# Zero products ahead of the first transform, paired butterflies, quartered fifth denominators and another tail order in a two-headed attention and Fourier kernel

## The chip, the cores and the metric

The kernel runs on one core of one Trainium2 chip. The metric is the device time of one execution in microseconds. Three runs of the kernel before gave 710.68, 712.03 and 708.92 us; their median is 710.68 us. A smaller time is better.

## The reference

Two independent computations share one launch, and their results stand side by side in the output (2048 x 1152).

```python
def _A_ref(x, wq, wk, wv, wo, beta):          # x: 1 x 2048 x 576, 32 heads of 18, 4 segments of 512
    q, k, v = heads(x @ wq), heads(x @ wk), heads(x @ wv)
    M = 0; z = 0
    for s in range(4):
        p = softmax(qs @ ks.T * scale + causal mask); a_dot = p @ vs
        pq = phi(qs); num = pq @ M; den = pq @ z + 1e-6
        outs.append(g * num / den + (1 - g) * a_dot)
        M = M + phi(ks).T @ vs;  z = z + phi(ks).sum(rows)
    return concat(outs) @ wo
def _B_ref(x, w_r, w_i):                      # x: 1 x 2048 x 576
    return irfft2(rfft2(x) * (w_r + 1j * w_i), s=(2048, 576))
```

Here phi(t) is t+1 for positive t and exp(t) otherwise, and g is the sigmoid of beta.

## The kernel before, in words

The order of the instructions on each engine is the order in which the Python code emits them: the tile framework's own scheduling is off. Every engine works through its own list in order. Generators are advanced by hand so that work of one part lies between work of another. The stages, by the profile's time, are:

- **Forward transform, 0 to 71 us** (class FFT, `forward`, L103 to L198). The 2048 rows are taken as 16 blocks of 128 (`u` = 0 to 15). For each block SyncE loads `xin`; `prep` (L121) forms sum and difference `eo` on VectorE, rounds them on ScalarE into `eh`, and forms the rest `el` on VectorE. `eh` lives in three buffers whose third part holds zeros beside 33 written rows; GpSimd clears these parts at the start (L166). `f1` (L136) multiplies the block with the table `ftab` on TensorE, 14 products for one block: for each of two results `r` two with the first half of the table, two with its second half, and two with `el`, and one with the small table `ftab2`. GpSimd issues the loads of the first half, the second half and `ftab2` (L170 to L173), after the clearing. The result is copied to `X` by ScalarE (L147) and VectorE (L150), multiplied by the twiddle matrices `cfw` (`c1`, L155, 12 products) and stored in `Z`. The loop at L181 emits this for `u`, `u-1` and `u-3` side by side.
- **Length-16 part of the transform on VectorE, spread over 36 to 324 us.** `bf` (L200) is a butterfly of four complex tiles of 2 x 290 elements, ten VectorE instructions: six on 580 elements and four on 290. `tws` (L211) multiplies by a twiddle: two ScalarE scalings of 580 (L218, L219) and two VectorE instructions of 290 (L224, L226) for one tile. `stage1` does this for each of four groups, `middle` runs a butterfly, the multiplication by the filter `W`, the inverse butterfly and the twiddles, and `last` one more butterfly. There are 16 butterflies and 18 twiddled tiles. A counter (`Pace`) hands their steps out: one or two for a block in the forward transform, and then an equal share for each unit of the projections.
- **Projections, 71 to 271 us** (L548). For each of four segments `g` nine units of q and k (`qk_unit`, L466) and four of v. In a q/k unit TensorE makes 14 products into `pj`, ScalarE and VectorE split the result into three bfloat16 parts `sp` (L477, L484, L491), TensorE subtracts the second part (L493), and ScalarE makes the third (L494).
- **Inverse transform, 271 to 350 us** (`inverse`, L285), with the first scores beside it.
- **Attention, 350 to 660 us** (L954). For each of 128 pairs of a segment and a head TensorE makes scores `s`, VectorE takes maxima, ScalarE exponentials `P`, and TensorE the products with v. Background generators run between them; one of them is `den` (L779), called three times. It multiplies `zst`, the sums of phi(k) laid out for five groups of heads `t`, with `pq` = phi(q): four groups into the four sets of 32 output rows of one accumulator `pd`, which ScalarE copies to `ds`; in its next step the fifth group into 32 rows of a new accumulator, with a copy of its own. SyncE then writes `ds` to memory, from where `recip` reads it back.
- **Tail, 660 to 708 us** (end of `attention`). Eight accumulators (`u`: four row blocks, two halves of 288 columns) collect the last output projection. `last_proj(u,t)` (L902) adds the three products of head group `t`. The parts `t`<4 are emitted for `u`<7, then for `u`=7; then a loop adds `t`=4 to each `u`, copies the half on ScalarE or VectorE (L1047), and after each second one SyncE writes a row block of 576 columns (L1048).

Of the kernel before, what the change touches and what calls it, by code (L numbers as in the profile page):

```python
# [5 lines left out]
F32=mybir.dt.float32; F32R=mybir.dt.float32r  # L6
AF=mybir.ActivationFunctionType; OP=mybir.AluOpType
# [95 lines left out]
class FFT:  # L103
# [4 lines left out]
    def forward(s,xp,cp,pp,wl,xs,consts):  # L108

        nc,io=s.nc,s.io; v=nc.vector  # L110
# [25 lines left out]
        def f1(u):  # L136
            p=pp.tile([128,2,512],F32,name="f1",tag="f1")
            h,l=eh.pop(u),el.pop(u)
            for r in range(2):
                L=[(h[:,r,0],tab[:,0,r,0]),(h[:,r,1],tab[:,0,r,1]),(h[:,r,0],tab[:,1,r,0]),(h[:,r,1],tab[:,1,r,1]),  # L140
                   (l[:,r,0],tab[:,0,r,0]),(l[:,r,1],tab[:,0,r,1]),(l[:99,r,2],tab2[:99,r])]
                for n,(x,t) in enumerate(L):
                    nc.tensor.matmul(p[:,r,:FP],x,t,start=n==0,stop=n==6)  # L143
            F[u]=p
        def ev0(u):
            x=xp.tile([128,2,FP],F32R,name="X0",bufs=3); X[u]=[x]
# [16 lines left out]
                        nc.tensor.matmul(p[:,r,:FP],cc[:,hl,k*128:(k+1)*128],x[i][:,q],start=n==0,stop=n==5)  # L163
                        n+=1
        H=[xp.tile([128,2,3,128],F32R,name=f"eh{i}",bufs=1) for i in range(3)]
        for h in H: nc.gpsimd.memset(h[:,:,2].bitcast(F32),0.0)  # L166
        load(0)
        tab=cp.tile([128,2,2,2,FP],F32R,name="ftab",bufs=1)
        tab2=cp.tile([128,2,FP],F32R,name="ftab2",bufs=1)
# [7 lines left out]
        for i in range(2):  # L177
            for x in p: next(x)
        load(3)
        s.pace=Pace(61+165+40)  # L180
        for u in range(20):  # L181
            p=prep(u+2) if u+2<16 else iter(())
            if 0<u<17: ev0(u-1)
# [12 lines left out]
            if u>13: s.pace.take(2)  # L196
        for _ in wl: pass
        for _ in xs: pass  # L198
    def bf(s,x,y,inv):

        v=s.nc.vector; tp=s.tp
        t=[tp.tile([128,2,FP],F32,name=f"t{i}",tag="t",bufs=8) for i in range(4)]
        p,m=(y[1],y[3]) if not inv else (y[3],y[1])
        for o,a,b,op in ((t[0],x[0],x[2],OP.add),(t[1],x[0],x[2],OP.subtract),(t[2],x[1],x[3],OP.add),(t[3],x[1],x[3],OP.subtract),
                         (y[0],t[0],t[2],OP.add),(y[2],t[0],t[2],OP.subtract),
                         (p[:,0],t[1][:,0],t[3][:,1],OP.add),(p[:,1],t[1][:,1],t[3][:,0],OP.subtract),
                         (m[:,0],t[1][:,0],t[3][:,1],OP.subtract),(m[:,1],t[1][:,1],t[3][:,0],OP.add)):
            v.tensor_tensor(o,a,b,op=op)  # L208
            yield
    def tws(s,L,inv):  # L210

        nc=s.nc; v=nc.vector; A=[]; L=[x for x in L if x[1]]
        if not L: return
        for i in range(len(L)+1):
            if i<len(L):
                y,e=L[i]; a=-2*np.pi*e/16*(-1 if inv else 1)
                t=[s.tp.tile([128,2,FP],F32,name=f"tw{k}",tag="t",bufs=8) for k in range(2)]
                nc.scalar.activation(t[0],y,AF.Copy,scale=float(np.cos(a)))  # L218
                nc.scalar.activation(t[1],y,AF.Copy,scale=float(np.sin(a)))  # L219
                A.append((y,t))  # L220
                if i==0: yield
            if i>0:
                y,t=A.pop(0)
                v.tensor_tensor(y[:,0],t[0][:,0],t[1][:,1],op=OP.subtract)  # L224
                yield
                v.tensor_tensor(y[:,1],t[0][:,1],t[1][:,0],op=OP.add)  # L226
                yield
    def stage1(s,b):
        x=[s.Z[:,b,a] for a in range(4)]
        yield from s.bf(x,x,False)  # L230
        yield from s.tws([(x[c],b*c) for c in (2,1,3)],False)
    def middle(s,wp):
        nc,io=s.nc,s.io; v=nc.vector
        Ws=[]
        def ld(i):
            W=wp.tile([128,2,FP],F32,name="W",bufs=3)
            nc.sync.dma_start(W,io["w"][i//4][:,i%4])
            Ws.append(W)
        for i in range(3): ld(i)
        for c in range(4):  # L240
            x=[s.Z[:,b,c] for b in range(4)]
            yield from s.bf(x,x,False)
            for d in range(4):
                W=Ws[4*c+d]
                t=s.tp.tile([128,2,FP],F32,name="wm",tag="t",bufs=8)
                t2=s.tp.tile([128,2,FP],F32,name="wm2",tag="t",bufs=8)
                v.tensor_tensor(t,x[d],W[:,0][:,None,:].to_broadcast([128,2,FP]),op=OP.mult)
                yield
                v.tensor_tensor(t2,x[d],W[:,1][:,None,:].to_broadcast([128,2,FP]),op=OP.mult)
                if 4*c+d+3<16: ld(4*c+d+3)  # L250
                yield
                v.tensor_tensor(x[d][:,0],t[:,0],t2[:,1],op=OP.subtract)
                yield
                v.tensor_tensor(x[d][:,1],t[:,1],t2[:,0],op=OP.add)
                yield
            yield from s.bf(x,x,True)
            yield from s.tws([(x[b],b*c) for b in (2,1,3)],True)
    def inv_setup(s,cp):
        nc,io=s.nc,s.io
        s.cp=cp; s.civ={}  # L260
# [9 lines left out]
    def last(s):  # L270

        for b in range(4):
            x=[s.Z[:,b,c] for c in range(4)]
            yield from s.bf(x,x,True)
# [69 lines left out]
BF=mybir.dt.bfloat16  # L344
# [43 lines left out]
class ATT:  # L388
# [123 lines left out]
    def v_unit(s,g,tb,tp,pp):  # L512
        nc=s.nc
        P=[]
        for hf in range(2):
            ps=pp.tile([128,288],F32,name="pjv",tag="pj")
            yield from s.passes(ps,g,"wv",slice(288*hf,288*hf+288),slice(128*tb,128*tb+128),True)
            P.append(ps)
            yield
        vt=tp.tile([128,622],F32,name="vt")  # L520
        vv=vt[:,:608].rearrange("p (h c) -> p h c",c=19)
        nc.gpsimd.memset(vv[:,:,18:19],1.0)  # L522
        nc.gpsimd.memset(vt[:,608:],0.0)
# [12 lines left out]
        n=g+1  # L536
        for t in range(5):
            w=7 if t<4 else 4; r=18*w
            m=tp.tile([126,7,19],F32,name="mm")
            nc.vector.tensor_tensor(m[:r,:w],s.pm[t//3][:r,t%3,:w],s.bm[:r,:w],op=OP.mult)  # L540
            M=s.Mst[n][:r,t,:r].rearrange("p (h c) -> p h c",c=18)
            z=s.zst[n][:r,t,:w]
            if n==1:
                nc.gpsimd.tensor_copy(M,m[:r,:w,:18])
                nc.gpsimd.tensor_copy(z,m[:r,:w,18])
            else:
                nc.gpsimd.tensor_tensor(M,m[:r,:w,:18],s.Mst[g][:r,t,:r].rearrange("p (h c) -> p h c",c=18),op=OP.add)
                nc.gpsimd.tensor_tensor(z,m[:r,:w,18],s.zst[g][:r,t,:w],op=OP.add)  # L548
    def projections(s,xp,tp,pp,wv,pace,hook):

        live=[]
# [6 lines left out]
        tot=pace.left-10  # L558
# [221 lines left out]
        s.pq[g,t]=x  # L780
    def den(s,g,lane):
        nc=s.nc; tp=s.tp
        ds,ds2=[tp.tile([128,512],F32,name=f"ds{i}",tag="ux",bufs=3) for i in range(2)]; ds2=ds2[:32]
        for T,d in ((range(4),ds),((4,),ds2)):
            pd=s.post("pd")
            for t in T:
                r=126 if t<4 else 72
                nc.tensor.matmul(pd[32*(t%4):32*(t%4)+32],s.zst[g][:r,t],s.pq[g,t][:r],start=True,stop=True,skip_group_check=True)
            nc.scalar.copy(d,pd[:d.shape[0]])
            yield  # L790
        for t in range(5):
            w=7 if t<4 else 4
            s.later(1,lambda t=t,w=w: nc.sync.dma_start(s.dD[g][7*t:7*t+w],ds[32*t:32*t+w] if t<4 else ds2[:w]))
# [147 lines left out]
    def attention(s,tp,ps):  # L941
# [6 lines left out]
        m=None  # L948
# [89 lines left out]
                if t==2 and u in (1,4): s.last_tile(3 if u==1 else 4,"rd")  # L1038
        s.last_low()
        for u in range(7): s.last_proj(u,3)  # L1040
        for t in range(4): s.last_proj(7,t)
        o=[s.tp.tile([128,4,512],F32,name=f"P{i}").rearrange("p a b -> p (a b)") for i in range(2)]
        o=[o[tb//3][:,576*(tb%3):576*(tb%3)+576] for tb in range(4)]
        nc=s.nc
        for u in range(8):
            tb,hf=divmod(u,2); s.last_proj(u,4)
            (nc.vector.tensor_copy if hf else nc.scalar.copy)(o[tb][:,288*hf:288*hf+288],s.acc[u])  # L1047
            if hf: nc.sync.dma_start(s.io["ya"][1536+128*tb:1664+128*tb],o[tb])  # L1048

def prio(tc,gen,off):  # L1050

# [104 lines left out]
```

## Time and profile before

| | |
|---|---|
| runs | 710.68, 712.03, 708.92 us (median 710.68) |
| profiled execution, own time | 709.86 us |
| its span, first to last instruction | 708.2 us |
| TensorE busy | 678.8 us, 96% of the span |
| VectorE busy | 544.8 us, 77% |
| ScalarE busy | 455.8 us, 64% |
| GpSimd busy | 194.6 us, 27% |
| granted TensorE clock, mean | 0.999 |

In the profile PE is TensorE (matmuls), PEld its weight loads, DVE VectorE, ACT ScalarE, POOL GpSimd and SP SyncE. A row of the timeline gives start, duration, engine, line, instruction, the tiles written and read, their shapes and the number of merged instructions; in brackets stands the idle time before it and what ended it. Durations of successive instructions overlap, so the distance between starts is what one of them costs the engine. A row of the table by windows gives for each engine the busy time in that stretch and the number of instructions, then the granted clock, the busy share of the DMA engines and the moved GB/s.

### The profile page before, as it was taken

The page shows a single profiled execution, that of the slowest core. Times are in us where ns is not written, and L with a number is a line of the kernel's source. Part 1 is how long each engine was busy: PE and PEld are TensorE (multiplying, and loading weights), DVE is VectorE, ACT ScalarE, POOL GpSimd, SP SyncE. Part 2 cuts the span into 40 slices and gives each one's busy share as a digit, 9 for nine tenths or more (in the row PEclk, how much of TensorE's full clock was granted, in tenths as well). Part 3 has the DMA queues.
Part 4 walks back from the last instruction along what each step waited for, and adds up shares of the span by engine and source line. Part 5 has one row for each costly group of instructions (what it writes and reads, how often), then busy time and mean ns, then how long its engine had stood idle before and what let it go on. Part 6 is the DMA issues. An engine that isn't in the chain of part 4 may idle for free.

```text
span 708.2 us, 14408 instructions
## 1 busy us (share of the span) xinstructions
PE 678.8 (96%) x4991; PEld 501.3 (71%) x4991; DVE 544.8 (77%) x1258; ACT 455.8 (64%) x1004; POOL 194.6 (27%) x392
## 2 busy tenths in 40 slices
PE   4999999999999999999999899999999999998997
PEld 3999769879779879998954454445566445663587
DVE  4899969899699789797787787988657876567533
ACT  3777796585686484544388777777656776567421
POOL 3111000100200102665135333444233752235310
PEclk9999999999999999999999999999999999999999
DMA  9897355666384679999338976976766766442151
GB/s 328 256 305 202 115 141 187 186 185 202 100 250 156 178 196 311 202 240 267 100 114 210 190 163 143 207 182 167 154 129 181 182 166 154 92 122 65 29 164 74
DMA packets 71146, 123.80 MB, mean 175 GB/s; under 512 B 12184, under 2 KB 39174, under 8 KB 67482
## 3 DMA queue, kind: packets, MB, share of 16 engines
q1 hardware_dynamic: 64422, 106.89, 57.4%
q0 software_dynamic: 5632, 15.76, 8.2%
q8 instruction: 39, 0.64, 0.4%
q10 hardware_dynamic: 1020, 0.25, 0.2%
q14 instruction: 33, 0.27, 0.1%
HBM read 82.10 MB, written 39.81 MB: 172 GB/s over the span
## 4 chain that ended last, share of the span: by engine, by line
PE 68%; DMA 8%; ACT 4%; DVE 4%; POOL 2%; issue 2%; SPq 0%; ACTq 0%; DVEq 0%; POOLq 0%
PE pj L464 12%; PE pv L734 9%; PE s L656 9%; PE pjv L464 8%; PE po L877 6%; PE i L309 3%; PE i L298 3%; PE s L705 3%; PE s L709 2%; DMA yb<-yout 2%; PE pn L807 2%; PE s L669 2%; PE pm L532 2%; PE s L714 2%; DMA Ks<-qkD 1%
## 5 line engine op out<-in xcount | busy, mean ns | idle before, releaser
L664 DVE CUSTOM_DVE_ANT_0 junk<-s,x 128x512 bf16<-128x512 f32 x248 | 137.0, 552 | 58.0 <-PE s L656 52.6
L719 POOL TENSOR_SCALAR_AFFINE_SELECT P<-P 128x512 f32<-128x512 f32 (+2 forms) x132 | 78.5, 626 | 112.9 <-ACT P L706 104.1
L670 DVE TENSOR_REDUCE mx<-s 128x4 f32<-128x512 f32 x128 | 87.7, 685 | 5.6 <-PE s L669 3.7
L706 ACT ACTIVATE P<-s 128x512 f32<-128x512 f32 x128 | 77.7, 607 | 10.8 <-PE s L705 3.8
L734 PE MATMUL pv<-P,vs 128*32 128x512 f32 (+3 forms) x1024 | 82.5, 439 | 0.1
L715 ACT ACTIVATE P<-s 128x256 f32<-128x256 f32 x128 | 49.8, 389 | 46.1 <-PE s L714 45.7
L711 ACT ACTIVATE P<-s 128x512 f32<-128x512 f32 x128 | 77.4, 605 | 2.4 <-PE s L710 2.2
L656 PE MATMUL s<-Ks,Qs 108*128 108x384 bf16 (+3 forms) x256 | 69.1, 301 | 1.5 <-DMA ux<-uD 1.0
L734 PEld LDWEIGHTS pv<-P,vs 128*32 128x32 f32 x1024 | 26.9, 109 | 45.3 <-issue 35.1
L464 PE MATMUL pj<-x,wqkh 128*128 128x512 f32 x162 | 56.5, 409 | 0.0
L208 DVE TENSOR_TENSOR Z<-t,t 128x290 f32<-128x290 f32 (+1 forms) x96 | 48.4, 553 | 0.1
L656 PEld LDWEIGHTS <-Qs 108*128 108x128 bf16 x320 | 31.5, 98 | 23.5 <-issue 12.1
L208 DVE TENSOR_TENSOR t<-Z 128x580 f32<-128x580 f32 x64 | 46.1, 755 | 0.0
L669 PE MATMUL s<-tri,idb 128*128 128x128 bf16 x256 | 43.0, 219 | 0.0
L522 POOL MEMSET vt<- 128x32 f32 x16 | 2.3, 162 | 141.3 <-PE pm L532 119.5
L298 PE MATMUL i<-civ,Y 128*128 128x256 f32 (+1 forms) x288 | 39.3, 289 | 0.2 <-POOL Y L283 0.2
L298 PEld LDWEIGHTS i<-civ,Y 128*128 128x128 f32 (+1 forms) x288 | 36.5, 181 | 1.0 <-POOL Y L283 0.4
L309 PE MATMUL i<-itab,T 128*128 128x290 f32 (+1 forms) x224 | 36.7, 306 | 0.5 <-DVE yout L317 0.4
L464 PE MATMUL pj<-x,wqkl 128*128 128x512 f32 x90 | 35.6, 395 | 0.0
L464 PE MATMUL pj<-xh,wqkl 128*128 128x512 f32 x90 | 35.5, 395 | 0.0
L143 PE MATMUL f<-ftab,eh 128*128 128x290 f32 x128 | 25.3, 321 | 10.7 <-DMA ftab<-ftab 10.6
L464 PE MATMUL pj<-xh,wqkh 128*128 128x512 f32 x90 | 35.5, 395 | 0.0
(210 smaller groups left out, 1806.3 us busy)
## 6 DMA issues: line engine op xcount, KB each, us to landing
qkD<-sp SPq DMA_DIRECT2D x32, 384.0 KB
xin<-xb SPq DMA_DIRECT2D x16, 384.0 KB
cfw<-cfw POOLq DMA_DIRECT2D x16, 384.0 KB, 4.7
civ<-civ POOLq DMA_DIRECT2D x16, 384.0 KB, 9.0
vs<-vD SPq DMA_DIRECT2D x16, 330.0 KB
vD<-vt SPq DMA_DIRECT2D x16, 311.0 KB
W<-w SPq DMA_DIRECT2D x16, 290.0 KB
yb<-yout SPq DMA_DIRECT2D x16, 290.0 KB
```

Source lines behind the costliest of these rows:

```text
L208: v.tensor_tensor(o,a,b,op=op)
L298: nc.tensor.matmul(p[:m,k],Y[i][:,q,c*128:c*128+m],cc[:,hl,o:o+256],start=n==0,stop=n==5)
L309: nc.tensor.matmul(p,x,t,start=n==0,stop=n==6)
L464: s.nc.tensor.matmul(out,a,b,start=i==0,stop=i==len(L)-1)
L656: nc.tensor.matmul(out,Q[:108,h,128*i:128*i+128],K[:108,h,:128*(i+1)],start=True,stop=True)
L664: nc.vector.tensor_tensor_reduce(out=junk[:,:w],in0=src,in1=s.mask[:,512-w:],scale=1.0,scalar=-3.0e38, op0=OP.add,op1=OP.max,accum_out=s.m ...
L669: nc.tensor.matmul(pa[:,o+w-128:o+w],s.idb,s.tri,start=False,stop=True,skip_group_check=True)
L670: nc.vector.tensor_reduce(out=s.mx[k][:,hh],in_=pa.rearrange("p (b c) -> p b c",c=128),axis=mybir.AxisListType.X,op=OP.max)
L706: nc.scalar.activation(P[0][:,hh],p0,AF.Exp,scale=SC)
L711: nc.scalar.activation(P[1][:,hh],p1,AF.Exp,scale=SC)
L719: nc.gpsimd.affine_select(out=x[:,r],in_=x[:,r],pattern=[[0,r.stop-r.start],[1,128]],compare_op=OP.is_ge,fill=0.0,base=0,channel_multiplie ...
L734: nc.tensor.matmul(s.pvt[32*hh:32*hh+32,128*j:],vt[:,j,19*h:19*h+32],mv[0][:,hh,mv[1]],start=j==0,stop=j>1,skip_group_check=True)
```

## The change

1. VectorE, not GpSimd, clears the three `eh` parts, after clearing a new tile `z`. TensorE multiplies `z` with itself 26 times ahead of the first transform, into a buffer of `c1`, and five times more inside block 0.
2. In block 0 the four products with the first half of the table come first for both results; then the five zero products; then the rest.
3. A butterfly writes its last two results with one instruction of 2 x 290 each (the third part is read in reverse order), so that it has eight instructions and not ten. Where a twiddle is a quarter turn (two tiles), the butterfly's subtraction does it, in two halves. The other 16 twiddled tiles have two ScalarE scalings of 290 and one VectorE `scalar_tensor_tensor` of 580. The counter's totals fall from 266 to 216.
4. The fifth group of denominators is added into the accumulator of the first four: columns 8 to 11 of each set of 32 rows, a quarter of the 512 query columns in each. One copy is left; SyncE writes the fifth group in four pieces.
5. In the tail the `t`<4 part of `u`=7 stands after `u`=5 is finished, and the last row block is written in two halves.

```diff
         def f1(u):
...
+            O=[(r,n) for r in range(2) for n in range(7)]
+            if u==0: O.sort(key=lambda a: a[1]>1)
+            for i,(r,n) in enumerate(O):
+                x,t=L[r][n]
+                nc.tensor.matmul(p[:,r,:FP],x,t,start=n==0,stop=n==6)
+                if u==0 and i==3: zeros(5)
...
-        for h in H: nc.gpsimd.memset(h[:,:,2].bitcast(F32),0.0)
+        z=xp.tile([128,512],BF,name="z",bufs=1)
+        v.memset(z,0.0)
+        def zeros(n):
+            for i in range(n): nc.tensor.matmul(zp[:,0],z[:,:128],z,start=True,stop=True)
+        for h in H: v.memset(h[:,:,2].bitcast(F32),0.0)
...
+        zp=pp.tile([128,2,512],F32,name="c1",tag="c1")
+        zeros(26)
-        s.pace=Pace(61+165+40)
+        s.pace=Pace(44+140+32)
...
     bf:
+        L=[(t[0],x[0],x[2],OP.add),(t[1],x[0],x[2],OP.subtract),(t[2],x[1],x[3],OP.add),(t[3],x[1],x[3],OP.subtract),(x[0],t[0],t[2],OP.add)]
+        if turn:
+            g,h=(t[2],t[0]) if inv else (t[0],t[2])
+            L+=[(y[:,0],g[:,1],h[:,1],OP.subtract),(y[:,1],h[:,0],g[:,0],OP.subtract)]
+        else: L+=[(y,t[0],t[2],OP.subtract)]
+        L+=[(s.slots(p,m+1),t[1],t[3][:,::-1],OP.add),(s.slots(m,p+1),t[1],t[3][:,::-1],OP.subtract)]
...
     tws:
+                for k in range(2): nc.scalar.activation(t[:,k],y[:,1-k],AF.Copy,scale=float((-np.sin(a),np.sin(a))[k]))
...
+                nc.vector.scalar_tensor_tensor(z,z,c,x,op0=OP.mult,op1=OP.add)
...
     den:
+        for t in range(4): nc.tensor.matmul(pd[32*t:32*t+32],s.zst[g][:126,t],s.pq[g,t][:126],start=True,stop=False,skip_group_check=True)
+        for j in range(4):
+            c=slice(128*j,128*j+128)
+            nc.tensor.matmul(pd[32*j:32*j+32,c],s.zst[g][:72,4],s.pq[g,4][:72,c],start=False,stop=True,skip_group_check=True)
+        nc.scalar.copy(ds,pd)
...
-        for t in range(4): s.last_proj(7,t)
...
+            if u==6:
+                for t in range(4): s.last_proj(7,t)
...
+            if hf or u>5: nc.sync.dma_start(s.io["ya"][1536+128*tb:1664+128*tb,c],o[tb][:,c])
```

TensorE's list begins with block 0 of the forward transform. Before, with `f` the accumulator, `eh` and `el` the block's parts and `ftab` the table:

```order
L143 MATMUL f_167<-ftab,eh_112 128x290 x4
L143 MATMUL f_167<-ftab,el 128x290 x2
L143 MATMUL f_167<-ftab_121,el 128x290
L143 MATMUL f_167<-ftab,eh_112 128x290 x4
L143 MATMUL f_167<-ftab,el 128x290 x2
L143 MATMUL f_167<-ftab_121,el 128x290
```

After it begins as follows (the pair of load and product with `z` stands 26 times ahead of `f` and five times behind its first four products):

```order
L172 LDWEIGHTS z
L172 MATMUL c_162<-z 128x512
L145 MATMUL f_196<-ftab,eh_112 128x290 x4
...
L145 MATMUL f_196<-ftab,eh_112 128x290 x2
L145 MATMUL f_196<-ftab,el 128x290 x2
L145 MATMUL f_196<-ftab_123,el 128x290
```

The four products that need only the first half of the table now come ahead of everything that needs the second half or the small table.

Also on TensorE, in the attention stage, the first call of `den` before (the scores `s` between its two steps make up 20 rows, the products with v two):

```order
L788 MATMUL pd<-pq,zst_67 32x512 x4
L656 LDWEIGHTS Qs_3306
L656 MATMUL s_5677<-Ks_3307,Qs_3306 128x256
...
L734 MATMUL pv<-P_5444,vs 32x384 x4
L734 MATMUL pv<-P_5445,vs 32x256 x4
L788 MATMUL pd<-pq,zst_67 32x512
```

And after:

```order
L722 MATMUL s_5625<-Qs_3267,x_2721 128x128
L797 MATMUL pd<-pq,zst_67 32x512 x4
L800 MATMUL pd<-pq,zst_67 32x128 x4
L668 LDWEIGHTS Qs_3268
L668 MATMUL s_5640<-Ks_3269,Qs_3268 128x256
```

The single product of 512 columns behind the products with v has become four of 128 columns directly behind the first four.

On VectorE, in the projections of segment 0, the end of the third group of `stage1` before, with `tw` the scaled copies, `pj`, `sp` and `ex` the work of the projection units and `xl`, `wvl` splits of loaded data:

```order
L208 TENSOR_TENSOR Z<-t_1050,t_1052 128x290
L410 TENSOR_TENSOR wvl<-raw,wvh 64x288
L437 TENSOR_TENSOR xl<-xst,xh 128x512
L224 TENSOR_TENSOR Z<-tw_1163,tw_1164 128x290
L483 SCALAR_TENSOR_TENSOR ex<-pj,ex 128x512
L484 TENSOR_TENSOR pj<-pj,sp_1183 128x512
L226 TENSOR_TENSOR Z<-tw_1163,tw_1164 128x290
L224 TENSOR_TENSOR Z<-tw_1188,tw_1189 128x290
L226 TENSOR_TENSOR Z<-tw_1188,tw_1189 128x290
```

And after:

```order
L225 TENSOR_TENSOR Z<-t_1018,t_1020 128x2x290 x2
L421 TENSOR_TENSOR wvl<-raw,wvh 128x288 x2
L448 TENSOR_TENSOR xl<-xst,xh 128x512
L495 TENSOR_TENSOR pj<-pj,sp_1140 128x512
L237 SCALAR_TENSOR_TENSOR Z<-Z,tw 128x580
L421 TENSOR_TENSOR wvl<-raw,wvh 128x288
L421 TENSOR_TENSOR wvl<-raw,wvh 64x288
L237 SCALAR_TENSOR_TENSOR Z<-Z,tw 128x580
L494 SCALAR_TENSOR_TENSOR ex<-pj,ex 64x512
```

The four halves of a butterfly's end have become two instructions, a twiddled tile has one and not two, and the third group's twiddles stand one to two units earlier.

More of the change, by code (lines that the diff above doesn't have):

```diff
@@ L240, in middle @@
         for c in range(4):
-            x=[s.Z[:,b,c] for b in range(4)]
-            yield from s.bf(x,x,False)
+            I=[8*b+2*c for b in range(4)]; x=[s.slots(i,i+1) for i in I]
+            yield from s.bf(I,False)
             for d in range(4):
@@ L255, in middle @@
                 yield
-            yield from s.bf(x,x,True)
-            yield from s.tws([(x[b],b*c) for b in (2,1,3)],True)
+            yield from s.bf(I,True,c==2)
+            if c: yield from s.tws([(I[b],b*c) for b in (2,1,3) if b*c!=4],True)
     def inv_setup(s,cp):
@@ L272, in last @@
         for b in range(4):
-            x=[s.Z[:,b,c] for c in range(4)]
-            yield from s.bf(x,x,True)
+            yield from s.bf([8*b+2*c for c in range(4)],True)
             s.done=b
@@ L557, in advance @@
                 except StopIteration: live.remove(l)
-        tot=pace.left-10
+        tot=pace.left-8
         for g in range(4):
@@ L782, in den @@
         nc=s.nc; tp=s.tp
[L783 to L793, printed above, removed]
+        ds=tp.tile([128,512],F32,name="ds",tag="ux",bufs=3)
+        pd=s.post("pd")
+        for t in range(4): nc.tensor.matmul(pd[32*t:32*t+32],s.zst[g][:126,t],s.pq[g,t][:126],start=True,stop=False,skip_group_check=True)
[3 more added lines that the diff above has]
+        nc.scalar.copy(ds,pd)
+        yield
+        for t in range(4):
+            s.later(1,lambda t=t: nc.sync.dma_start(s.dD[g][7*t:7*t+7],ds[32*t:32*t+7]))
+        for j in range(4):
+            s.later(1,lambda c=slice(128*j,128*j+128),j=j: nc.sync.dma_start(s.dD[g][28:32,c],ds[32*j+8:32*j+12,c]))
+        yield
         def chain():
```

59 lines of the change are left out of this document (25 added, 34 removed).

## The prediction

> **What bounds the kernel now.** I read the busy times first, then the waits of TensorE stage by stage, then the timeline where it waits.
>
> ```profile
> PE 678.8 (96%) x4991; PEld 501.3 (71%) x4991; DVE 544.8 (77%) x1258; ACT 455.8 (64%) x1004; POOL 194.6 (27%) x392
> 40.00:60.00 20.00, 19.88 (x140) 18.75 (x139) 19.92 (x32) 14.82 (x27) 3.34 (x7) 1.00 0.85 258
> 90.00:110.00 20.00, 18.33 (x98) 14.55 (x97) 14.46 (x27) 18.74 (x36) 0.00 (x0) 1.00 0.51 140
> 110.00:271.00 161.00, 160.29 (x925) 136.81 (x924) 139.40 (x261) 106.05 (x207) 14.26 (x60) 1.00 0.63 186
> ```
>
> TensorE is the bound nearly everywhere. So an edit pays where it takes TensorE's own work away, where TensorE waits, or ahead of its first and behind its last product. Work taken from VectorE or ScalarE pays only where these are full: VectorE from 40 to 60 us (19.92 of 20), ScalarE from 90 to 110 us (18.74 of 20).
>
> The opening is the largest hole. TensorE's rows, and one of its weight loads:
>
> ```profile
> 9.62 0.82 PE L143 MATMUL f<-ftab,eh 128*128 128x290 f32 x2 [9.62 <-DMA ftab<-ftab]
> 11.38 0.85 PE L143 MATMUL f<-ftab,eh 128*128 128x290 f32 x2 [0.93 <-DMA ftab<-ftab]
> 12.66 0.29 PEld L143 LDWEIGHTS f<-ftab,el 99*128 99x128 f32 x1 [0.31 <-DMA ftab<-ftab]
> 13.07 1.17 PE L143 MATMUL f<-ftab,eh 128*128 128x290 f32 x4
> 14.77 1.17 PE L143 MATMUL f<-ftab,eh 128*128 128x290 f32 x4
> 16.46 1.03 PE L143 MATMUL f<-ftab,eh 128*128 128x290 f32 x4
> 17.72 0.71 PE L143 MATMUL f<-ftab,eh 128*128 128x290 f32 x4
> 21.52 1.79 PE L163 MATMUL c<-X,cfw 128*128 128x290 f32 x12
> 37.22 0.70 PE L143 MATMUL f<-ftab,eh 128*128 128x290 f32 x4
> 40.73 0.69 PE L143 MATMUL f<-ftab,eh 128*128 128x290 f32 x4
> ```
>
> It waits 9.62 us for the first half of the table, 0.93 for the second, and then runs slowly: seven products take 1.70 us (13.07 to 14.77), 0.243 each. Later a block's 26 products (14 of `f`, 12 of `c`) take 3.51 us (37.22 to 40.73), 0.135 each. The granted clock reads 1.00 in the windows, so that column does not show it; the distances do. Four products have 1.03 us at 16.46 and 0.71 at 17.72: the fast rate comes at about 16.9 us, 5.5 us after the last gap.
>
> **The opening in the change.** A product of 512 bfloat16 columns at the fast rate costs 0.22 us:
>
> ```profile
> 508.20 0.38 PE L705 MATMUL s<-Qs,x 110*128 110x512 bf16 x1
> 508.42 0.38 PE L656 MATMUL s<-Ks,Qs 108*128 108x512 bf16 x1
> 0.81 0.81 POOL L166 MEMSET eh<- 128x256 f32 x3 [0.29 <-POOLq L1143]
> 1.56 0.72 POOL L170 DMA_DIRECT2D ftab<-ftab  x1
> ```
>
> Slowly it would cost 0.22 x 0.243/0.135 = 0.40 us. The zero products wait for `z`, cleared from about 0.8 to 1.2 us if VectorE is about as quick as GpSimd (0.81 us for three). Fourteen slow ones fill the 5.5 us until 6.7, twelve fast ones 2.6 us more: they end at 9.3 us, just ahead of the table's 9.62. Behind them four products (0.54) and five zeros (1.1) reach 11.3; the second half lands at 11.38, the small table at 12.66. The last six of block 0 then end at about 13.6 us, not 14.77. Three more blocks of 14 x 0.135 = 1.89 us end at 19.3, where `c` stood at 21.52: TensorE gains 2.2 us. `z` holds one of two `c1` buffers until 11.3; the second `c` comes long after.
>
> What is late next is VectorE, which forms `el`:
>
> ```profile
> 13.62 1.03 DVE L126 TENSOR_TENSOR eo<-xin 128x384 f32<-128x384 f32 x2 [1.21 <-DMA xin<-xb]
> 15.01 0.64 ACT L147 CAST X<-f 128x580 fp32r<-128x580 f32 x1 [3.59 <-PE f L143]
> 15.67 0.62 ACT L129 CAST eh<-eo 128x512 fp32r<-128x512 f32 x1
> 16.75 0.96 DVE L133 TENSOR_TENSOR el<-eo,eh 128x768 fp32r<-128x768 f32 x1 [0.31 <-ACT eh L130]
> 23.76 1.02 DVE L126 TENSOR_TENSOR eo<-xin 128x384 f32<-128x384 f32 x2
> 27.50 1.02 DVE L126 TENSOR_TENSOR eo<-xin 128x384 f32<-128x384 f32 x2
> 43.54 0.75 DVE L150 TENSOR_TENSOR X<-f,X 128x580 fp32r<-128x580 f32 x1
> 44.35 0.81 PE L143 MATMUL f<-ftab,eh 128*128 128x290 f32 x4
> ```
>
> A block takes TensorE 3.51 us (37.22 to 40.73), but VectorE 3.74 (23.76 to 27.50); from 44.35 on TensorE starts a block only when VectorE's `X` frees an accumulator (43.54 + 0.75 = 44.29). So the stage ends when VectorE's chain lets it, and that chain begins with block 3's `eo` at 13.62, which waits for data. Behind it ScalarE was held by the copy of `X` until 15.65. From its rounding to `el` pass 1.08 us (15.67 to 16.75). With block 0 done at 13.6 the copy is over at 14.3, ScalarE rounds at 14.65, and `el` starts at 13.62 + 1.03 + 1.08 = 15.73: 1.0 us earlier. The lead of 2.2 us shrinks to that within some five blocks.
>
> Against it stands the moved clearing: GpSimd's table loads can be issued 0.75 us earlier (1.56 to 0.81), while the transfer engines are full. If the table goes ahead, `xin` comes later. [...] I take 0.1, since the table's half a megabyte has other data ahead of it in any case, and count **0.9 us** (0.3 to 2.2; the upper end if VectorE's chain moves as far as TensorE).
>
> **Butterflies.** Distances on VectorE and ScalarE's twiddles:
>
> ```profile
> 36.58 0.75 DVE L208 TENSOR_TENSOR t<-Z 128x580 f32<-128x580 f32 x1
> 37.25 0.95 DVE L133 TENSOR_TENSOR el<-eo,eh 128x768 fp32r<-128x768 f32 x1
> 97.38 0.45 DVE L226 TENSOR_TENSOR Z<-tw,tw 128x290 f32<-128x290 f32 x1
> 97.75 0.45 DVE L224 TENSOR_TENSOR Z<-tw,tw 128x290 f32<-128x290 f32 x1
> L218 ACT ACTIVATE tw<-Z 128x580 f32<-128x580 f32 x18 | 12.4, 692 | 4.5 <-DVE Z L208 4.5
> L879 ACT COPY ob<-po 128x288 f32<-128x288 f32 x24 | 9.5, 399 | 19.6 <-PE po L877 17.2 <-DMA ya<-ob 1.9
> PE pj L493 <- ACT sp L491: 2.2, 3, 1.0
> ```
>
> A full instruction costs 0.67 us, a half 0.37. Sixteen butterflies trade four halves (1.48) for two full (1.34): 2.2 us less. Eighteen twiddles of two halves (13.3) become 16 of one full (10.7): 2.6 less; the two turned ones give 0.1 back. VectorE loses 4.7 us. ScalarE, with two halves of about 0.4 us (the nearest row, L879) for two of 0.69, goes from 24.8 to 12.8 us. Nearly all of it lies beside TensorE, which is 99% busy from 110 to 271 us. What can be won is TensorE's wait for `sp`: 2.2 us in three places. A new arrangement makes new waits, so I count a third, **0.7 us** (-0.5 to 2.2). Two small waits in the inverse transform are left at nothing. The counter deals 2.5 steps to a unit where it dealt 3.2; none waits for more than its neighbours.
>
> **Tail.**
>
> ```profile
> 702.61 2.75 SPq L1048 DMA_DIRECT2D ya<-P  x4
> 705.00:706.00 1.00, 0.00 (x0) 0.00 (x0) 0.00 (x0) 0.00 (x0) 0.00 (x0) 1.00 0.90 346
> 706.00:707.00 1.00, 0.00 (x0) 0.00 (x0) 0.00 (x0) 0.00 (x0) 0.00 (x0) 0.83 0.63 244
> ```
>
> TensorE's last product and the last copy stand where they did. But four writes of 0.29 MB leave within 2.75 us and still move at 706.6. The first three now start 12 products (1.6 us) earlier, and the last issue carries a half, 0.15 MB: at 346 GB/s 0.4 us less. **0.4 us** (0 to 0.8).
>
> **Denominators.** Their rows on TensorE, each with its successor:
>
> ```profile
> 510.05 1.04 PE L788 MATMUL pd<-pq,zst 126*32 126x512 f32 x8
> 511.03 0.28 PE L656 MATMUL s<-Ks,Qs 108*128 108x256 bf16 x1
> 512.41 1.04 PE L788 MATMUL pd<-pq,zst 72*32 72x512 f32 x2
> 513.39 0.28 PE L656 MATMUL s<-Ks,Qs 108*128 108x256 bf16 x1
> ```
>
> Four groups cost 0.98 us, and the fifth alone 0.98 as well: products into different sets of 32 rows run beside each other, and the fifth has only one set. In quarters it has all four and 128 columns each, 0.98/4 = 0.25 us. That is 0.73 us of TensorE's own work, three times: **2.2 us** (0, if quarters run one behind the other, to 2.2). One ScalarE copy in each call goes too, beside other work. SyncE issues three writes more for a call, ahead of the read that `recip` waits for, at most 3 x 0.69 us by the tail's four in 2.75; they are handed over one step earlier than now, which covers it, and I take nothing.
>
> **Sum.** 0.9 + 0.7 + 2.2 + 0.4 = 4.2 us. From the profiled execution's 709.86 us that gives 705.7; from the runs' median of 710.68, 0.8 above it, 706.5. I forecast **706.0 us**. A measurement can tell 0.5%, 3.55 us, from no change: below 707.1 is faster, above 714.2 slower.
>
> **Rivals.**
> *The zero products leave the slow rate as it is* (0.06). Nothing here shows products of zeros at the start. Then 26 x 0.40 end at 11.6 us, four products at 12.6, five zeros at 14.6 and ten products at 17.0, where block 0 ended at 14.77; ScalarE's copy and `el` come 2.2 us later than before: 709.86 + 2.2 - 3.3 = 708.8. For it speaks only that the rate is not in the clock column. [...]
> *Only TensorE's own work counts* (0.18): `xin` comes later by as much as ScalarE is freed, and the new order of twiddles makes as many waits as it takes away. 2.2 + 0.4 leave 707.3 to 708.1, so 707.7.
> *The quarters don't run beside each other* (0.06), and the change does not do there what it says: 4.2 - 2.2 = 2.0 less, 708.3.
> *VectorE takes a paired instruction as slowly as two full ones* (0.05), because of reversed or jumping operands. In the projections 32 of 0.67 us grow by as much, 21 us, less the 4.7. VectorE idles 161 - 139.4 = 22 us from 110 to 271 and about 5.5 from 90 to 110. It decides once a window of some units is full, as from 40 to 60 us, where TensorE follows VectorE; if half of the 17 us falls there, 709.86 + 8.5 - 3.5 = 714.9: slower. Against it: no row here has such operands slower, but none has a reversed one.
> *All waits go* (0.05): 2.2 + 2.2 + 2.2 + 0.8 = 7.4 less, 702.5.
>
> **How the numbers follow.** My forecast has 0.60; within its bounds nine in ten lie below 707.1 (0.54), the rest above. With *all waits go* (0.05) and a sixth of *only TensorE's work* (0.03) faster has 0.62. Slower has the paired instructions, 0.04, and 0.01 of the first rival. The rest, 0.33, is no change. The range leaves out *all waits go*, the paired instructions and half of the first rival: 703.8 to 708.9.
>
> **What would show it.** Right: zero products from about 1.2 us, at first 0.40 and later 0.22 us apart; block 0 at 0.135 us for one product; VectorE's `el` of block 3 at 15.7 to 16.1 us; the stage still led by VectorE, about 0.9 us earlier; fifth denominators of 0.25 us; paired instructions of 0.755 us; the last write issued at the same distance from TensorE's last product. Wrong: real products still 0.243 us apart, `eo` of block 3 later than 14.4 us, four quarters of 0.9 us together, a new wait of TensorE in the projections of over 1 us.

## The result, and the profile after

The changed kernel takes 705.49 us (median of six runs, 703.38 to 705.81) where the kernel before took 710.39 in the runs beside it: a ratio of 0.9936, 95% interval 0.9911 to 0.9961. In two later sets it stood at 0.9915 (0.9885 to 0.9945) and 0.9912 (0.9883 to 0.9942). The forecast of 706.0 us and its range hold. The parts do not: two that were forecast small or not at all turn out the largest, and they pull opposite ways.

The profiled execution took 705.81 us (span 704.1). First its busy times, from the page:

```profile
span 704.1 us, 14447 instructions
...
PE 682.5 (97%) x5040; PEld 503.3 (71%) x5040; DVE 540.4 (77%) x1212; ACT 444.9 (63%) x997; POOL 193.3 (27%) x389
```

VectorE has 4.4 us less to do and ScalarE 10.9 less. TensorE has 49 products more, and its span is 4.1 us shorter. The timeline of TensorE in the opening (start, duration, line, operation):

```profile
1.26 7.85 PE L172 MATMUL c<-z 128*128 128x512 bf16 x26 [1.26 <-DVE z L170]
8.76 0.89 PE L145 MATMUL f<-ftab,eh 128*128 128x290 f32 x4
9.49 1.25 PE L172 MATMUL c<-z 128*128 128x512 bf16 x5
...
11.98 0.71 PE L145 MATMUL f<-ftab,eh 128*128 128x290 f32 x4
...
14.99 0.81 PE L145 MATMUL f<-ftab,eh 128*128 128x290 f32 x4 [0.94 <-DVE X L153]
...
18.06 0.81 PE L145 MATMUL f<-ftab,eh 128*128 128x290 f32 x4 [0.90 <-DVE X L153]
```

The zeros start at 1.26 us. By the starts in the trace they stand 0.43 us apart until 5.49 us and 0.22 from there on, so the fast rate came while nothing but zeros ran. Block 0 is over at 11.98 instead of 14.77, with block products 0.135 us apart. Then TensorE waits for VectorE in two places, and its lead shrinks as was forecast. VectorE's chain from block 3 on, with 2.20 us from `eo` to `el` where it was 3.13:

```profile
13.23 1.03 DVE L126 TENSOR_TENSOR eo<-xin 128x384 f32<-128x384 f32 x2 [1.33 <-DMA xin<-xb]
...
15.43 0.96 DVE L133 TENSOR_TENSOR el<-eo,eh 128x768 fp32r<-128x768 f32 x1 [0.50 <-ACT eh L130]
```

Next the end of the FFT stage. ScalarE's rows, then TensorE's (`c` is the last step of the FFT, `pj` the first projection):

```profile
69.32 0.63 ACT L157 COPY Z<-c 128x580 f32<-128x580 f32 x1
71.27 0.78 ACT L234 ACTIVATE tw<-Z 128x290 f32<-128x290 f32 x2 [1.31 <-DVE Z L225]
71.96 0.62 ACT L157 COPY Z<-c 128x580 f32<-128x580 f32 x1
```

```profile
68.76 1.64 PE L166 MATMUL c<-X,cfw 128*128 128x290 f32 x11
72.63 0.73 PE L475 MATMUL pj<-x,wqkh 128*128 128x512 f32 x2 [2.23 <-ACT Z L157]
...
74.45 1.05 PE L475 MATMUL pj<-x,wqkh 128*128 128x512 f32 x2
...
75.73 1.05 PE L475 MATMUL pj<-x,wqkh 128*128 128x512 f32 x2
...
77.54 0.63 PE L475 MATMUL pj<-x,wqkh 128*128 128x512 f32 x2
```

This is new: TensorE, done with `c` at 70.4 us, waits 2.23 us for the last copy of `Z`, and from 74.45 to 77.0 two products take 1.05 us where they take 0.63 later. In between the granted clock is 0.50 (a row of the table by windows):

```profile
74.00:75.00 1.00, 1.00 (x4) 0.78 (x3) 1.00 (x3) 0.59 (x3) 0.00 (x0) 0.50 0.00 0
```

The waits of TensorE in the rest of the projections (74 to 280 us), which were 2.2 us in three places, are one:

```profile
PE pj L504 <- ACT sp L502: 0.4, 1, 0.4
```

The three denominators, on TensorE's timeline of the first:

```profile
426.89 1.06 PE L797 MATMUL pd<-pq,zst 126*32 126x512 f32 x8
427.78 0.40 PE L800 MATMUL pd<-pq,zst 72*32 72x128 f32 x8
428.11 0.28 PE L668 MATMUL s<-Ks,Qs 108*128 108x256 bf16 x1
```

All five groups take 1.22 us (426.89 to 428.11), where they took twice 0.98. At the end, VectorE's last copy, and SyncE's issues of the last output writes, five where there were four:

```profile
700.91 0.46 DVE L1062 COPY P<-po 128x288 f32<-128x288 f32 x1 [2.00 <-PE po L920]
```

```profile
697.43 4.31 SPq L1063 DMA_DIRECT2D ya<-P  x5
```

From the last copy to the end of the span it is 704.1 - 700.91 = 3.2 us.

To see where time came from, I took the start of the same product of TensorE in both profiles and subtracted (after minus before; a negative number is earlier). The steps between two such places add up to the whole:

| stretch (us in the kernel before) | step, us | what stands there |
|---|---|---|
| to the last `c`, 71.4 | -1.33 | opening |
| to the first `nid` product of the projections, 79.7 | +4.04 | wait for `Z`, slow products |
| to the end of the projections, 280 | -2.96 | butterflies |
| inverse, to 355 | +1.86 | a wait of 1.9 for `yout`, where there was 0.4 |
| 355 to 421, attention | -0.50 | waits for transfers |
| three denominators, 421 to 632 | -0.78, -0.82, -0.75 | |
| 632 to the first product of the last projection, 686.5 | -1.63 | `rrD` is read back 1.85 us after its write, not 3.13 |
| to its last product, 704.1 | -0.71 | a wait of 0.29 for `rd` is gone; the rest is not traced |
| to the end of the span | -0.47 | tail |

### The profile page after: what moved, and what is told of

The parts are those of the page before. It is cut to its first block, busy times and chain, and to the rows that moved or that the text cites. A ratio compares the mean times of both kernels' runs of the same rounds, so it can differ in the third digit from the quotient of the medians.

```text
span 704.1 us, 14447 instructions
## 1 busy us (share of the span) xinstructions
PE 682.5 (97%) x5040; PEld 503.3 (71%) x5040; DVE 540.4 (77%) x1212; ACT 444.9 (63%) x997; POOL 193.3 (27%) x389
## 4 chain that ended last, share of the span: by engine, by line
PE 80%; DMA 7%; DVE 5%; ACT 4%; issue 3%; POOL 2%; ACTq 0%; DVEq 0%; POOLq 0%; SPq 0%
PE pj L475 15%; PE pv L746 9%; PE s L668 9%; PE pjv L475 8%; PE po L891 7%; DMA yb<-yout 4%; PE f L145 4%; PE s L717 3%; PE c L166 3%; PE i L320 3%; PE i L309 3%; PE s L721 3%; PE po L920 2%; PE pn L821 2%; PE pm L543 2%
## 5 line engine op out<-in xcount | busy, mean ns | idle before, releaser
L225 DVE TENSOR_TENSOR Z<-t,t 128x580 f32<-128x580 f32 (+1 forms) x66 | 46.5, 738 | 0.1
L475 PEld LDWEIGHTS pj<-x,wqkh 128*128 128x128 f32 x162 | 31.1, 193 | 9.2 <-ACT Z L157 2.5
L494 DVE SCALAR_TENSOR_TENSOR ex<-pj,ex 128x512 f32<-128x512 f32 (+1 forms) x28 | 19.3, 688 | 22.6 <-ACT ex L492 22.4
```

Source lines behind the costliest of these rows:

```text
L475: s.nc.tensor.matmul(out,a,b,start=i==0,stop=i==len(L)-1)
```

## The experiments

Each kernel's time is a median of its runs; its ratio is to the kernel before in the same set, with its 95% interval. The steps are those of the table above, each from the one profiled execution.

**Holding the butterfly steps back.** My first theory was that the twiddle copies, which now stand on ScalarE ahead of the last `Z` copy, make the new wait.

```diff
-            if u>13: s.pace.take(2)
+            if 13<u<18: s.pace.take(2)
```

> The changed kernel with the two butterfly steps of the last two units of the FFT loop (units 18 and 19) held back until the projections. Theory A (the 2.23 us wait of TensorE at the first projection comes from twiddle copies that stand on ScalarE ahead of the last copy of Z, and the slow products behind it come from that wait): the wait falls under 0.5 us, the first projection products stand about 0.24 us apart at once, and all of the 3.8 us that were lost there come back: about 701.7 us. Theory B (the loss at the boundary only moves waits that come anyway: VectorE is behind by then, and the waits of TensorE for sp, 0.4 us in the changed kernel, come back to about 2.2 us as in the kernel before): about 703.5 us. Theory C (the boundary wait has another cause, such as the first weights or VectorE alone): the wait stays near 2.2 us and the time at 705.5 us.

Measured: 703.44 us, 0.9899 (0.9874 to 0.9924). That can't be told from the changed kernel in the same set (703.87, below), so the times decide nothing here; the profile does. The copy now goes first, but the wait does not vanish. ScalarE, then TensorE:

```profile
72.01 0.64 ACT L157 COPY Z<-c 128x580 f32<-128x580 f32 x1 [0.48 <-PE c L166]
...
72.83 0.79 ACT L234 ACTIVATE tw<-Z 128x290 f32<-128x290 f32 x2
```

```profile
72.70 0.74 PE L475 MATMUL pj<-x,wqkh 128*128 128x512 f32 x2 [0.73 <-ACT Z L157]
```

So the twiddles are 1.5 of the 2.23 us. The other 0.73 has another cause: in the kernel before, `pj` began at 71.57 us without waiting for that copy at all, which began at 71.77.

**The changed kernel again.**

> The changed kernel once more, for a second profile beside the others of this chip. Theory A: the 2.23 us wait at the first projection is set by the order of the program and stands again within 0.3 us, as do the three denominators at 1.22 us; the wait for yout near 338 us (1.9 us) and the 1.85 us between writing and reading back the last rows of rrD are times of transfers and may differ by 1 us or more. Theory B: these two stand again as well, and so belong to the change. Time 705.5 us by both.

Measured: 703.87 us, 0.9915 (0.9885 to 0.9945). The wait of 2.23 us stands again, but no slow products behind it:

```profile
73.57 0.73 PE L475 MATMUL pj<-x,wqkh 128*128 128x512 f32 x2 [2.23 <-ACT Z L157]
74.14 0.40 PE L475 MATMUL pj<-x,wqkl 128*128 128x512 f32 x1
74.37 0.63 PE L475 MATMUL pj<-x,wqkh 128*128 128x512 f32 x2
```

The boundary costs +2.49 here, not +4.04. The wait for `yout` is 1.5 us and not 1.9, and a wait of 1.7 us for a write of `uD` in the attention was not in the first profile. These two belong to the execution, the 2.23 us to the program. Behind the wait for `uD` the granted clock falls to 0.50 from 400.5 to 403.9 us; wait and slow clock together make most of a step of +2.6 between 355 and 421 us:

```profile
401.00:402.00 1.00, 1.00 (x8) 0.32 (x10) 0.74 (x2) 0.61 (x2) 0.00 (x0) 0.50 0.97 199
```

The early read back of `rrD` stands again, and so by the expectation's own test it goes with the program. It comes 1.85 or 1.86 us after the write in all eight executions of the changed kernel, with and without hold, two tiles or four buffers, 1.88 to 2.24 in the four that leave out the opening or the denominators, and 3.10 to 3.13 in the kernel before and with the butterflies alone. Why is open. In those eight the step from 632 to 681 us is -0.8 to -1.0.

**The butterflies alone, and the opening alone**, each put into the kernel before (the diff's parts 3, and 1 with 2).

> The kernel before with the butterflies in pairs alone (new steps, new totals of the counter; no zero products, old denominators, old tail). Theory A: the boundary wait of about 2.2 us and the slow products behind it appear here too, and outweigh the sp waits of the projections that go (2.2 to about 0.4 us): +1.1 us by the alignment of the two traces at 280 us, about 711.5 us. Theory B (the prediction's term): the butterflies bring 0.7 us, about 709.7 us.

> The kernel before with the opening alone (26 and 5 zero products, third units cleared by VectorE, new order in the first block). Theory A: 1.3 us, as the two traces stand apart at the end of the FFT stage, and all of it is kept to the end: about 709.1 us. Theory B (the prediction's term): 0.9 us, 709.5 us. Theory C: what is gained at the opening is lost at the boundary with the projections, where VectorE and ScalarE set the start: 710.4 us.

Measured: the butterflies alone 707.55 us, 0.9965 (0.9945 to 0.9985); the opening alone 710.03, 1.0005 (0.9983 to 1.0028). With the butterflies alone the time lies below both theories, since no wait stands at the boundary. The opening alone comes nearest its theory C, but not by C's cause: of the 2.0 us that its profile is ahead at the last `c`, the boundary takes 1.0, and more goes in the inverse and the attention, where the waits vary. With the butterflies alone, the twiddles stand ahead of the last `Z` copy just as in the changed kernel, and TensorE does not care. ScalarE, then TensorE:

```profile
73.23 0.78 ACT L225 ACTIVATE tw<-Z 128x290 f32<-128x290 f32 x2 [1.31 <-DVE Z L216]
73.92 0.62 ACT L154 COPY Z<-c 128x580 f32<-128x580 f32 x1
```

```profile
72.21 0.63 PE L466 MATMUL pj<-x,wqkh 128*128 128x512 f32 x2
```

`pj` starts 1.7 us ahead of the copy's start. With the opening alone there are no twiddles ahead, and TensorE waits for the copy (69.75 to 70.40) all the same:

```profile
69.75 0.65 ACT L157 COPY Z<-c 128x580 f32<-128x580 f32 x1 [0.49 <-PE c L166]
```

```profile
70.45 0.73 PE L473 MATMUL pj<-x,wqkh 128*128 128x512 f32 x2 [0.74 <-ACT Z L157]
```

What the opening has to do with this place, 60 us later, is the accumulator of the zeros. `zp` is a tile of `c1`, which has two buffers in turn. One tile more at the start, and each of the 16 real `c` falls on the other buffer than before. The first projection's accumulator lies where one of the two lay: before, that was the last `c` but one, copied out early; now it would be the last.

**Two tiles for the zeros** test that: the 26 write the first, the five write the second, and the real `c` are back in their old places.

```diff
-        zp=pp.tile([128,2,512],F32,name="c1",tag="c1")
-        zeros(26)
+        zp,zq=[pp.tile([128,2,512],F32,name="c1",tag="c1") for k in range(2)]
+        zeros(zp,26)
...
-                if u==0 and i==3: zeros(5)
+                if u==0 and i==3: zeros(zq,5)
```

> The changed kernel with two accumulator tiles c1 taken for the zero products (26 write the first, five the second) where it takes one, so that the c1 buffers of the real products fall on the same two places as in the kernel before. Theory A (the one tile for the zeros shifts the c1 buffers by one place, and only by that do the first projection products lie where the last Z copy still reads; the twiddle copies ahead of that copy make the wait longer but don't cause it): the wait of 2.2 us at the first projection product falls under 0.3 us although the twiddle copies still stand ahead of the last Z copy; 2.2 us less than the changed kernel on this chip (703.9 us): 701.7 us. Theory B (the twiddles alone cause it, the place of the buffer does not matter): the wait stays at 2.2 us, 703.9 us.

> The kernel with two tiles for the zero products, and with the butterfly steps of units 18 and 19 held back as well. Theory A: without the shared place there is nothing left for the hold to gain, so the time is that of the kernel with two tiles, 701.7 us, and no wait for Z at the first projection. Theory B: only the two together take the wait away; then this one alone stands at 701.7 us. Theory C: the four steps that are held back delay VectorE in the projections and bring sp waits back, up to 1 us later: 702.7 us.

Measured: two tiles 700.97 us, 0.9868 (0.9841 to 0.9895), the best of all. TensorE, then ScalarE:

```profile
66.77 3.25 PE L166 MATMUL c<-X,cfw 128*128 128x290 f32 x23
69.87 0.63 PE L475 MATMUL pj<-x,wqkh 128*128 128x512 f32 x2
```

```profile
70.89 0.79 ACT L234 ACTIVATE tw<-Z 128x290 f32<-128x290 f32 x2 [1.31 <-DVE Z L225]
71.59 0.62 ACT L157 COPY Z<-c 128x580 f32<-128x580 f32 x1
```

`pj` follows `c` with no wait, though the twiddles still stand ahead of the copy at 71.59: the shifted buffer is the condition, the twiddles only the amount. With the hold added the boundary is as clean (a step of 0.00 in both), at 703.07 us, 0.9911 (0.9880 to 0.9943). So the hold gains nothing more. That it costs 2 us is not shown: two of the nine runs, at 706.88 and 709.98 with mean granted clocks of 0.998 and 0.993 (1.000 in all four with two tiles alone), carry much of the difference, and its profile has -3.22 in the projections where two tiles alone have -2.97.

**All but the opening.**

> The changed kernel without its opening (no zero products, GpSimd clears the third units, first block in the order of before); butterflies, denominators and tail as changed. Theory A (the opening gains 0.4 to 1.3 us up to the end of the FFT stage and costs 2.2 us or more at the boundary through the shifted buffers): no wait at the first projection product, and 0.9 to 1.8 us faster than the changed kernel: about 702.5 us. Theory B (the prediction's sum, by which the opening brings 0.9 us to the end): 704.8 us.

Measured: 703.07 us, 0.9908 (0.9877 to 0.9939), and no wait for `Z`. Leaving the opening out loses nothing against the changed kernel, so there it was worth nothing; once the buffers are right the medians put it at about 2 us (703.07 against 700.97 in one set), but their intervals overlap, and part of this may be the clock: it falls to 0.50 twice in the profile without the opening, behind waits of 1.8 us for `yout` and 2.1 us for `uD`.

**The denominators undone**, in the changed kernel and, in a later set, in the one with two tiles.

> The changed kernel with the fifth denominator product as before (a step of its own, with its own eviction). By the prediction each of the three denominators costs 0.73 us more again, so the alignment with the changed kernel falls back by 0.7 to 0.8 us at each of three places after 421 us and the time is 2.2 us above it: about 706.1 us. Rival (TensorE's time there is taken up by waits that come anyway): steps of under 0.3 us, 704.5 us or less.

> The kernel with two tiles for the zero products and the old denominators (fifth product a step of its own with its own eviction). By the prediction's term 2.2 us above the kernel with two tiles: 703.2 us. Theory B (the first comparison, 709.0 us, holds: the denominators are worth some 4 us in the runs, since more than TensorE's 0.73 us each hangs on them): 705 us. Steps of the alignment at the three denominators: 0.75 to 0.82 us each by both, and under B a further loss at a place that can be named.

Measured: 709.02 us, 0.9986 (0.9964 to 1.0009), and 704.82, 0.9924 (0.9900 to 0.9948). In that second set the kernel with two tiles stands at 702.09, so the old denominators cost 2.7 us. By the steps, the three places at 421 to 632 us are worth -0.01, +0.01 and 0.00 in the first and -0.05, +0.02 and -0.01 in the second, where the kernels with the new denominators have -0.75 to -0.86 at each, 2.35 us together in the first profile. A further loss of 0.90 and 0.42 us stands between 456 and 494 us in these two profiles, away from the denominators; it is 0.47 with the opening alone, whose denominators are old too, nothing with the butterflies alone, and at most 0.01 in all nine profiles with the new ones. What makes it is not shown. Why the first of the two was 5 us above the changed kernel's two later sets is not settled either. The clock is likely a part of it, since eight of its ten runs list a mean granted clock of 0.998 or less; the other two took 706.89 and 707.67 us. The second does not repeat it.

**The last set: the two kernels side by side, and four buffers for `yout`** (`bufs=3` to `bufs=4` in the kernel with two tiles).

> The kernel with two tiles for the zero products once more, beside the changed kernel in the same set. Theory A (shifted buffers cost the changed kernel 2.2 us and what slow products follow): 0.3 to 0.6% below the changed kernel, 700.5 to 702 us. Rival (its first runs were lucky in their transfers): the same as the changed kernel, 704 us.

> The changed kernel, beside its variants. By both theories 704 to 705.5 us, with the 2.2 us wait at the first projection product; a third look at what follows that wait: if products 0.42 us apart follow it again or not, in 0 to 3.4 us.

> The kernel with two tiles for the zero products, and four buffers instead of three for the results yout of the inverse. Theory A (TensorE's waits for yout in the inverse, 0.3 to 1.9 us in six of the nine profiles, come from writes of yb that end late and give their buffer back late): no wait for yout is left between 280 and 352 us, and the time is about 0.8 us lower on average: 700.2 us. Rival (the delay only moves to the next buffer or queue): 701 us as with three buffers.

Measured: two tiles 702.09 us, 0.9887 (0.9862 to 0.9912); the changed kernel 703.62, 0.9912 (0.9883 to 0.9942). The difference of 1.5 us, 0.2%, has the expected sign but falls short of the expected 0.3 to 0.6%, and the intervals overlap; the profile carries the claim, with a wait of 2.23 us in all four executions with shifted buffers and twiddles ahead, and none in all five with two tiles. Slow products followed the wait in one of those four. With four `yout` buffers: 701.02 us, 0.9878 (0.9852 to 0.9905), no wait for `yout`; but that execution of three buffers had none either, so nothing is decided.

## Why the prediction was right, and where it was not

**Opening (forecast -0.9 us; up to 71.4 us it is -1.33 in the first profile).** The mechanism was right: the fast rate comes while only zeros run (0.43 us apart, and 0.22 from 5.49 us on), TensorE's lead of 2.8 us at block 0 is not kept, and VectorE's chain sets the stage. It does so exactly. In all eleven profiled executions with the new opening, the last `c` starts 56.86 to 56.88 us after block 3's `eo` (13.23 and 70.11 in the first), even with the hold, where TensorE's clock is at 0.50 from 17.1 to 20.5 us. In the three without it, it is 57.81 (the kernel before: 13.62 and 71.43), 58.38 (butterflies alone) and 56.86 (no opening, where the first half of the table came earliest, at 9.19 us against 9.62 and 9.44). So at equal arrival of data the opening is worth 0 to 1.5 us, 0.8 on average, about the forecast's 0.9, and mostly it makes the stage steady. Against the kernel before it is 0.94 us, and 0.93 of it lie between that `eo` and its `el`, where the forecast had put 1.0. The rest is when `xin` lands: `eo` starts anywhere from 12.37 to 14.80 us in these executions, and the stage ends that much earlier or later. The 0.1 us that the forecast took for a later `xin` was my estimate, and no run shows it: the runs show this spread of 2.4 us and no delay of `xin` on average (`eo` at 13.3 us in eleven with the new opening, 13.7 in three without).

**The step that failed: "`z` holds one of two `c1` buffers until 11.3; the second `c` comes long after."** I asked when the buffer comes free, and not what one turn more does to all that follows. It moves every later `c` to the other buffer, up to the stage's last, which the next stage's first accumulator lies over. That is 0.73 us alone (opening alone, hold) and 2.23 with the twiddles ahead. The forecast's own list of what would make it wrong had "a new wait of TensorE in the projections of over 1 us"; it came, though the butterflies alone don't make it.

**"None waits for more than its neighbours" failed with it.** With fewer steps in a butterfly the counter reaches a group's twiddles before the FFT loop ends, and on ScalarE the last `Z` copy, behind them in its list, stands behind a wait of 1.31 us for VectorE: in the first profile `c` is done at 70.4 us, the twiddles start at 71.27 and the copy at 71.96. Alone that costs nothing, as the butterflies alone show.

**Butterflies (forecast -0.7): the term was mis-sized by a factor of four.** From 79.7 to 280 us the step is -2.96 in the changed kernel, -2.94 with the butterflies alone, -2.98 without the opening, -2.97 with two tiles, and -0.09 with the opening alone. I had 2.2 us of waits as the most that could go, and took a third for fear of new ones. The listed waits fell from 2.2 to 0.4, nearly all. The other 1.1 us were never in the list. TensorE's rows of the kernel before show one listed wait and three that the list does not have:

```profile
192.08 0.38 PE L493 MATMUL pj<-sp,nid 128*128 128x512 bf16 x1 [0.56 <-ACT sp L491]
195.32 0.40 PE L464 MATMUL pj<-x,wqkh 128*128 128x512 f32 x1
195.68 0.38 PE L493 MATMUL pj<-sp,nid 128*128 128x512 bf16 x1
199.29 0.38 PE L493 MATMUL pj<-sp,nid 128*128 128x512 bf16 x1
202.90 0.38 PE L493 MATMUL pj<-sp,nid 128*128 128x512 bf16 x1
```

The `nid` products stand 3.60 to 3.61 us apart, and 3.48 to 3.49 with the butterflies alone: each round loses 0.12. The loss lies just ahead of the `nid` product. It starts 0.36 us after the product before it (195.32 to 195.68), and 0.24 after it with the butterflies alone. But the record of one product is 0.40 us long and covers the start of the next, so no idle time is seen; the listed waits hide some 0.15 us each in the same way. From 161 to 211 us the step is -1.08, where the list has 0.56.

**Denominators (forecast -2.2).** Right in mechanism and size: 0.98 + 0.98 became 1.22, and the steps are -2.35 in all. **Tail (forecast -0.4).** From the last product to the end of the span there is 0.47 us less in the first profile, 0.48 with two tiles and 0.46 without the opening, and none with the butterflies alone.

**Not forecast, and different from execution to execution:** waits in the inverse and for transfers. In the inverse the wait for `yout` was 0.4 us before and 1.9, 1.5 and 0 in the three profiles of the changed kernel; over the other executions it lies from 0 to 1.8. That late writes cause it is not shown. In the attention a wait for writes of `uD` or `rD`, of 1.2 to 2.1 us, appears in some and not in others. In the second profile of the changed kernel, where the granted clock falls behind such a wait, the two make most of a step of +2.6 us. The early read back of `rrD` was not forecast either, but it is steady from execution to execution.

So the total came out partly by luck. In the first profile the forecast's four terms make -7.1 us and not -4.2, and the places that it did not have make +3.1: a butterfly term 2.3 us too small stood against a boundary of +2.5 us or more that nobody had counted. Opening, denominators and tail were right for the reasons given.

## What to carry to other kernels

A buffer taken once, early, from a rotating pair costs no waiting where it is taken, and may cost it where the pair is last used (0.73 to 2.23 us here): count which buffer the last user gets and what is laid over it next. A list of waits is a lower bound for what a less loaded engine gives back, because a wait can hide under the overlap of two products (0.12 us in each round here); compare the distance of repeated rounds instead. Where one arrival sets a stage, compare kernels from that arrival on, and the noise of transfers falls out (a spread of 2.4 us became one of 0.02 in the eleven executions with the new opening). Behind a long wait, look at the granted clock before all of the loss is put down to the wait (2.49 us without a fall and 4.04 with one here).

## What the runs showed of the hardware

The granted clock fell to 0.50 in mid-kernel six times in the fourteen profiles, for 3.41 us each: at 73.7 us in the first profile after, at 17.1 with the hold, 400.5 in the second profile of the changed kernel, 395.8 with two tiles and hold, and 334.8 and 416.7 without the opening. By the trace's clock record each fall comes a whole number of steps of 3.413 us after the clock first opened in that execution (20, 3, 116, 114, 94 and 118 steps). In the step just ahead TensorE had been idle for 2.23, 1.83, 1.96, 1.50, 1.77 and 1.87 us. The same wait of 2.23 us at the boundary did no such thing in three other executions: there an edge of a step cut it in two, and no step held more than 1.61 us of it. Waits of 1.5 us for `yout` in the second profile of the changed kernel, of 1.6 for `T` with the hold and of 1.7 for `yout` with the butterflies alone brought no fall either, and no fall came behind less than 1.50. The idle times rest on modelled ends of products, and what makes the clock fall is not shown.

Ahead of the first opening the clock's column reads 1.00 even where the zeros stand 0.43 us apart, because the record begins only there (at 5.47 us in the first profile after). TensorE's rows in the held kernel, idle for 1.83 us and then slow:

```profile
16.55 0.91 PE L145 MATMUL f<-ftab,eh 128*128 128x290 f32 x4 [1.83 <-DVE X L153]
...
17.98 1.17 PE L145 MATMUL f<-ftab,eh 128*128 128x290 f32 x4
...
21.06 0.70 PE L145 MATMUL f<-ftab,eh 128*128 128x290 f32 x4
```

So a wait of 2.23 us at the boundary cost 2.49 to 2.50 us in three executions, and 4.04 in the one where the clock fell behind it.
